# DeltaNet and a low-rank mixer on one core: the diagonal blocks of K K^T picked by ScalarE copies in five of eight units, with all queue orders drawn anew

## The chip, the cores and the metric

The kernel runs on one core of one Trainium2 chip. The metric is the time of one execution on the device, in microseconds (us). Engines: TensorE (PE, with its weight loads PEld), VectorE (DVE), ScalarE (ACT), GpSimd (POOL) and SyncE (SP), which only issues DMAs here. A verdict compares the medians of several executions of two kernels on the same chip.

## The reference

Two blocks follow each other: a DeltaNet recurrence over 4 batches, 8 heads, 768 tokens and head dimension 48, and a mixer over 384 channels with a low-rank token step (rank 32) and a two-layer channel step (384 to 1536 to 384). All in fp32.

```python
def _attn_ref(q, k, v, beta):
    k_n = k / (np.linalg.norm(k, axis=-1, keepdims=True) + 1e-06)
    state = np.zeros((B, H, D, D), dtype=np.float32)
    for t in range(S):
        kt, vt, bt = (k_n[:, :, t], v[:, :, t], beta[:, :, t, None])
        y[:, :, t] = np.einsum('bhd,bhde->bhe', q[:, :, t], state)
        v_old = np.einsum('bhde,bhd->bhe', state, kt)
        state = state + bt[:, :, :, None] * np.einsum('bhd,bhe->bhde', kt, vt - v_old)

def _moe_ref(x, U, V, w_ch1, w_ch2):
    xt = x.transpose(0, 2, 1)
    h = xt @ U @ V
    u = x + h.transpose(0, 2, 1)
    ch = np.maximum(u @ w_ch1, 0.0) @ w_ch2
    return u + ch
```

## The kernel before

**Units.** The recurrence is computed in chunks of 64 tokens (L = 64). A unit n (0 to 7) is half a batch: six chunks of all eight heads. Two slots of SBUF hold the units in turn. For each unit the kernel does this:

- `load` and `load_blocks`: DMAs of k, q, v and a second copy of k (called z), on the queues of SP and GpSimd.
- `norms`: norms of k, and the scaling of v.
- `grams(n, 0)` and `grams(n, 1)`: k (and q) are turned so that the head dimension lies on the partitions (TensorE transposes L668, or 32x32 VectorE transposes L690 in units 5 to 7), and TensorE forms K K^T (and K Q^T) per chunk in `products`, L704, for j = 0 and j = 1 (half of the heads each). A result is a [128, 2, 6, 64] block in two banks of PSUM (a "pair"). Of K K^T, each chunk's two 32x32 diagonal blocks are needed first. Rows sit in quarters of 32 partitions: quarters 0 and 2 hold the upper half of a chunk's rows, quarters 1 and 3 the lower half. So the upper diagonal block is columns 0 to 31 of quarters 0 and 2, the lower one columns 32 to 63 of quarters 1 and 3. They are collected in the tile `diag`: before, ScalarE multiplies columns 0 to 31 by a column `even[:, 0]` that is 1 in quarters 0 and 2 and 0 elsewhere (L714), and VectorE adds columns 32 to 63 times `even[:, 1]` (1 in quarters 1 and 3), in two instructions, r = 0 and 1 (L717). Then ScalarE copies the whole product to SBUF (L725).
- `blocks`: VectorE transposes `diag` into `gs` (L781), scales it, and inverts the 32x32 unit-triangular blocks by substitution, 31 steps of two instructions each (L790, L796; 15 steps in units 0 to 2, which split the blocks further). `joins` and `diagonals` then build the 64x64 inverses with small TensorE products, ScalarE copies (L926, L914) and GpSimd clears (L933).
- `recur(b)`: the 12 chunks of a batch in turn, each a chain from TensorE to VectorE or ScalarE and back: L1066 or L1107 (state times k), L1078 or L1120 (VectorE subtracts), L1090 and L1099 (ScalarE copies, units 2 to 7), L1135 (the update) and L1147 (VectorE adds it to the state). `outputs` and `put` (L972, L986, L956) give the chunk's rows of the mixer's input X.

**Mixer.** 12 blocks of 256 tokens. `front` does the low-rank step (L1469, L1486, added by VectorE in L1495) and transposes. The first seven blocks run `wide`: `channels`, six pieces each (L1580, or L393 in another form), a ReLU on ScalarE (L1545), then `narrow`, seven products with VectorE sums (L1695 or L393, added to X by VectorE in L1620). The last five blocks form the first layer in `products_of` (L1430) with fewer, precombined products. Weights come as fp64 bit patterns and are converted by VectorE and ScalarE in `convert` (L1244 to L1272). Results are stored by the SP queue (L1626, L1629).

**Order.** Nothing is scheduled at run time. Each part above is a generator that yields one step at a time, with the engine and a planned cost. The dictionary `ORDER` lists, for each engine, the number of the part whose step comes next; the loop `run` issues the steps in just that order, so each engine's queue is fixed. Parts are numbered as they are begun: 4 to 7 are `recur`; 8 to 11 are `norms`, `grams` for k, `grams` for q and `blocks` of unit 0, and 18 to 21, 30 to 33, 38 to 41 and so on by eight those of units 1, 2, 3 and on; `load` parts lie between them; 78 is the weights' load and conversion; 81 to 92 are `front`; 93 to 97 the first layer of the last five blocks; 98 to 109 `wide`. A number with points is a part begun by a part (39.0.0.0 is a `products` of unit 3, 102.2 the third `channels` piece of block 4). `PARTED` names the TensorE steps that are issued in quadrants: a 128x128 matmul is split into four of 64x64, which TensorE can interleave with the recurrence's 64-row products without a change of form.

The lines touched by the change are these: L714 and L717 in `products`; the steps that need its result, L781 (`blocks`) and L725; and all the strings of `ORDER`, with `PARTED`.

Of the kernel before, what the change touches and what calls it, by code (L numbers as in the profile page):

```python
# [15 lines left out]
L = 64  # L16
BK = 32
# [9 lines left out]
def kernel(  # L27
# [20 lines left out]
    nc = tc.nc  # L48
# [50 lines left out]
    def act(n):  # L99
        return 0.16 + n / 1200.0  # L100
# [27 lines left out]
    def advance(i, value, at):  # L128
# [20 lines left out]
        9.0 9.1 9.0.0.0 9.1.0.0 2*2 19.0 19.1 3 19.0.0.0 3 19.1.0.0 10.0 10.1 10.0.0.0 20.0 11.4 10.1.0.0  # L149
        11.4 11.2*2 11.4*2 11.2*2 20.1 11.4*4 20.0.0.0 11.2*4 20.1.0.0 4.1 4.0*2 4.1 21.2*2 4 4.4 21.2 4  # L150
        21.2 4.5 4 21.4*2 21.2 4 4.5 4.6 4*2 21.2 4.6 21.2*2 4.7 4*2 4.8 4.7 4 21.4 4.9 4 21.4 4 4.9 4.8
        4.2*2 21.4*2 4 4.10 21.4*2 4*2 4.10 4.11 4*2 4.11 4.3 32.0 31.0 4.3 31.1 4.12 4 31.0.0.0 31.1.0.0 4
        4.12 32.1 4.13 4*2 4.13 4.14 4 4.15 4 4.14 4.15 79 32.0.0.0 81 32.1.0.0 81*2 40.0 82 98.0*2 39.0
        39.1 82 98.1 40.1 39.1.0.0 39.0.0.0 98.1 98.2 33.2*2 98.2 98.3*2 98.4 33.4*2 33.2 98.4 33.2 98.5
        33.4*2 33.2*2 98.5 98.7 83 33.2 33.4 33.2 33.4 98.7 33.4*2 98.8 5 5.0 5 40.1.0.0 5 98.8 5.1 5 98.9 5
        98.9 5 5.1 98.9 5 98.9 5.2 5 98.10 5 5.2 5.3 5 99.0 5 99.0 5 5.3 5.4 5 99.0 5 99.0 5.5 5 99.1*2 5
        5.4 99.1*2 5.5 40.0.0.0 5 83 99.2*2 99.3*2 99.4 48.0 99.4 41.2*2 47.0 99.7 47.1 47.0.0.0 47.1.0.0
        41.4*2 99.5*2 48.1 41.2 41.4*2 41.2 99.7 99.8 48.1.0.0 5 99.8 5.6 5 48.0.0.0 5 99.9 5 99.9 5.7 5*2
        99.9 5 5.6 99.9 5.8 5.7 5 99.10 5*2 100.0 5.9 5 100.0 5.8 5 100.0 5 100.0 5.9 5 5.10 5 100.1 5.11 5
        5.10 100.1 5 5.11 100.1*2 84 100.2*2 100.3*2 100.4*2 100.5 100.7 100.5 49.2*2 55.0.0.0 84 55.1.0.0  # L160
        100.7 100.8 49.2 49.4*2 49.2 100.8 84 100.9*2 6 85 100.9 6 100.9 56.0.0.0 56.1.0.0 6 100.10 49.4*2
        6.0 6 101.0*2 85 6.1 6 101.1*2 6 101.1 6 101.1 6.2 6 101.2*2 6.1 6 101.2*2 6 6.3 6.2 101.3 6 101.3 6
        6.4 6.3 6 101.4 6 101.4 6.5 6 101.4 6 101.4 6.4 6 6.5 101.5*2 101.7*2 57.2*2 57.4*2 86 57.4*2 57.2*2
        101.8*2 101.9*2 63.0.0.0 101.10 6 101.10 6 63.1.0.0 102.0*2 86 6.6 6 102.1*2 64.0.0.0 6 6.6 102.2 6
        102.2 6.7 6 102.2*2 6 6.7 102.3 6 102.3 6.8 6 102.3 6 102.3 6.9 6 102.4 6 102.4 6.8 6 102.4 6 102.4
        6.10 6 102.5*2 6.9 6.11 102.5 6 102.5 6.10 6 102.7 6.11 102.7 87 102.7*2 64.1.0.0 87 102.8*2 102.9*2
        102.10 71.0.0.0 103.0*2 71.1.0.0 103.1*2 103.2*2 103.3*2 65.4*2 65.2*2 103.4*2 72.1.0.0 65.2*2
        65.4*2 103.5*2 87 103.7 7 72.0.0.0 7 103.7 7 7.0 103.8*2 7.1 7 103.8*2 7 88 7 103.9*2 7 7.1 7.2 7
        103.10 7 7.2 104.0 7 104.0 7.3 7 104.0*2 7 7.3 7.4 104.1 7 104.1 7 104.1*2 7.5 7 7.4 104.2 7 104.2
        88 104.3*2 7 7.5 73.4*2 73.2*2 104.4*2 104.5 73.4*2 73.2*2 104.5 7 104.7 7 7.6 7 104.7 7 7.7 104.8  # L170
        7.6 7 104.8 7 104.8 7 104.8 7 7.7 7.8 7 104.9 7 7.8 7.9 7 104.9 7 89 7 104.10 7 7.9 7.10 7 7.11 7
        104.10 7 7.10 7.11 79 93.2 93.1 79 89 93.4 93.2 93.1 93.3 93.2 93.3 93.4 93.1 93.5 93.1 93.2 93.1
# [12 lines left out]
        78.20*2 21.4 78.21 21.4 78.21*4 4 78.22*2 4 78.22*2 4 78.22 4 78.23*2 4 78.23*3 78.24*5 4 78.25*2
        31.0.0.0*2 31.1.0.0*2 4 33 4 30 4 78.25 4 33*2 4 78.25*2 33*2 78.26 32.0.0.0 78.26 81 33 78.26 81
        32.1.0.0*2 78.26 33 78.26 33 82 33*2 32.0.0.0 30 33*8 33.4 33.2 78.26.1*3 39.0.0.0 78.27 98.2.1*3
        39.1.0.0 78.26.1 39.0.0.0 30 78.27*4 39.1.0.0 33.2*3 33.4*2 78.27.1 33.4 41 98.5.1*2 78.27.1*2
        98.7.0 98.5.1 78.27.1 38 83 41 98.6 5 98.7.1 41*3 38 98.8.0 5 98.8.1 41*3 5 41 5 41*2 40.1.0.0
        98.9.0 41 98.9.1 5 40.1.0.0 41 98.10.0 5 41*2 5 41 5 41*2 5 41 5 41*15 41.2 5 99.2.1 40.0.0.0 99.2.1  # L190
        38 40.0.0.0 99.2.1 99.7.0 41.4 47.0.0.0*2 47.1.0.0*2 49 99.5.1*3 46 49*2 46 49*2 99.7.1 99.8.0 99.6
        5 48.1.0.0*2 99.8.1 49*2 48.0.0.0 5 48.0.0.0 49 5 49*2 5 49*2 5 99.9.0 49*2 99.9.1 49 99.10.0 5 49 5
        49*2 5 49 5 49*2 5 49 5 49*9 46 49*2 84 49 100.2.1*2 49.2 49.4 55.1.0 55.0.0 100.5.1*2 100.2.1
        100.5.1 100.7.0 84 55.1.0.0 55.0.0.0 55.1.0.0 100.7.1 55.0.0.0 100.6 57 100.8.0 54 100.8.1 56.0.0
        57*4 56.1.0 6 85 100.9.0 56.0.0.0 56.1.0.0 56.0.0.0 6 57 56.1.0.0 100.9.1 100.10.0 57*7 6 57 6 57*2
        6 57*2 6 57*3 101.2.1 57 6 57 6 57*2 6 57 6 57*5 6 54 57*3 57.2 101.2.1 101.7.0 57.4 101.2.1
        101.5.1*3 101.7.1 54 86 101.6 101.8.0 101.8.1 63.0.0 64.0.0 101.9.0 101.9.1 63.1.0 63.0.0.0 6
        63.0.0.0 101.10.1 101.10.0 64.1.0 63.1.0.0*2 65 62 65*2 6 65 64.0.0.0 62 6 64.0.0.0 65*2 6 65*2 6
        65*3 6 65 6 102.2.1 65 6 65 6 65*3 6 102.2.1*2 65 6 65 102.5.1*2 65 62 87 65 102.5.1 102.7.0 65*3
        102.7.1 65 102.8.0 65 102.6 102.8.1 87 65 102.9.0 65 71.0.0 65 102.9.1 102.10.0 64.1.0.0*2 71.1.0  # L200
        65*4 71.1.0.0 65 71.0.0.0 65.4 71.0.0.0 71.1.0.0 65.2 73 72.1.0 72.0.0 70 73*2 72.1.0.0 103.2.1 73
        72.1.0.0 73*3 103.2.1*2 73 103.7.0 103.5.1*2 72.0.0.0 73 7 103.5.1 103.7.1 73 72.0.0.0 7 73 103.6
        73*2 7 103.8.0 88 103.8.1 73 7 73*2 103.9.0 73*2 7 73 103.10.0 103.9.1 7 73*2 7 73*2 7 73*2 70 7
        73*3 7 73*6 73.2 73.4 7 70 80*3 104.2.1*2 80 104.2.1 104.5.1 7 80*2 93.0*2 104.5.1 7 104.7.0 104.5.1
        104.7.1 7 104.6 7*2 93.0 104.8.0 104.8.1 7 93.0 104.9.0 7 80 7 104.9.1 7 89 93.0 7*2 93.0*2 80
        93.0*2 80*2 93.0 80 104.10.0 80 93.2.1 94.0*3 80 93.1.1 93.0 80 93.3.1 93.2.2 93.1.2 93.1.3 104.10.1
        93.2.3 93.5.0 94.0 93.1.4 94.0*6 93.4.1 90 94.2.1 90 105.0*3 94.3.1 94.1.1 105.1 94.1.2 94.2.2
        105.1*2 105.3.1 105.3.0 95.0 94.1.3 95.0*4 94.5.0 94.2.3 95.0 105.4.0 94.0 105.2 94.4.1 95.0 105.4.1
# [209 lines left out]
    def quarter(i, size=BK):  # L418
        return slice(BK * i, BK * i + size)
# [1357 lines left out]
```

## Time and profile before

| quantity | us |
|---|---|
| median of 3 runs | 591.36 |
| lowest, highest | 589.72, 591.92 |
| profiled execution, its own time | 589.15 |
| its span in the trace | 587.4 |
| TensorE busy | 545.3 |
| VectorE busy | 456.2 |
| ScalarE busy | 227.3 |
| GpSimd busy | 118.1 |

How to read it: the span is from the first to the last event of the profiled execution, and the execution's own time has a little around it. A busy time is the time in which at least one instruction of the engine runs; TensorE's is the time of matmuls, whose weight loads (PEld) run beside them. The row of 40 digits cuts the span into slices of 14.7 us and gives the busy share in tenths; the row PEclk gives the clock that TensorE was granted, in tenths of full speed. An entry such as "PE P L972 <- DVE s L1147: 1.4, 3, 1.0" says that matmuls of line 972 waited 1.4 us in all, in 3 places, the longest 1.0 us, for VectorE's line 1147. Two instructions of one engine may overlap by some 0.1 us, so two instructions of 0.41 us can take 0.74 us together.

### The profile page before, as it was taken

The page shows a single profiled execution, that of the slowest core. Times are in us where ns is not written, and L with a number is a line of the kernel's source. Part 1 is how long each engine was busy: PE and PEld are TensorE (multiplying, and loading weights), DVE is VectorE, ACT ScalarE, POOL GpSimd, SP SyncE. Part 2 cuts the span into 40 slices and gives each one's busy share as a digit, 9 for nine tenths or more (in the row PEclk, how much of TensorE's full clock was granted, in tenths as well). Part 3 has the DMA queues.
Part 4 walks back from the last instruction along what each step waited for, and adds up shares of the span by engine and source line. Part 5 has one row for each costly group of instructions (what it writes and reads, how often), then busy time and mean ns, then how long its engine had stood idle before and what let it go on. Part 6 is the DMA issues. An engine that isn't in the chain of part 4 may idle for free.

```text
span 587.4 us, 25542 instructions
## 1 busy us (share of the span) xinstructions
PE 545.3 (93%) x11460; PEld 491.1 (84%) x11460; DVE 456.2 (78%) x1086; ACT 227.3 (39%) x483; POOL 118.1 (20%) x205
## 2 busy tenths in 40 slices
PE   5697778799999999999999999999999999999997
PEld 4586677588888987997897798988889999999997
DVE  6898999999899898899878888888547574555552
ACT  4447476544433623344344305324423422131220
POOL 8132050311205304340252253301000000000000
PEclk9576666799999999999999999999999999999999
DMA  9634676652104314223212433200000000000013
GB/s 157 85 76 128 192 188 166 134 91 63 29 4 83 68 22 83 74 53 63 48 30 61 80 75 71 60 29 3 2 5 1 2 1 1 1 2 1 1 42 119
DMA packets 79213, 35.17 MB, mean 60 GB/s; under 512 B 65600, under 2 KB 76992, under 8 KB 79104
## 3 DMA queue, kind: packets, MB, share of 16 engines
q1 hardware_dynamic: 71200, 24.10, 18.9%
q0 software_dynamic: 6304, 9.15, 7.2%
q8 instruction: 90, 1.47, 1.0%
q10 hardware_dynamic: 1600, 0.30, 0.3%
q14 instruction: 19, 0.16, 0.1%
HBM read 28.80 MB, written 4.72 MB: 57 GB/s over the span
## 4 chain that ended last, share of the span: by engine, by line
PE 79%; DVE 7%; ACT 5%; DMA 4%; issue 3%; SPq 1%; POOL 1%; DVEq 0%; ACTq 0%; POOLq 0%
PE P L1695 24%; PE P L1580 12%; PE P L1430 12%; PE P L393 10%; PE P L704 3%; DMA wide<-in_moe_w_ch_dram 2%; PE P L668 2%; PE P L1066 2%; PE P L1090 1%; PE P L972 1%; PE P L1486 1%; PE P L986 1%; PE P L1135 1%; PE P L1514 1%; PE P L861 1%
## 5 line engine op out<-in xcount | busy, mean ns | idle before, releaser
L1695 PE MATMUL P<-w_sb,hs 128*128 128x192 f32 x480 | 84.2, 329 | 0.1
L1580 PE MATMUL P<-ut,w_sb 128*128 128x256 f32 x348 | 81.8, 386 | 0.1
L1695 PEld LDWEIGHTS P<-w_sb,hs 128*128 128x128 f32 x480 | 77.7, 190 | 1.3 <-issue 0.3
L1580 PEld LDWEIGHTS P<-ut,w_sb 128*128 128x128 f32 x348 | 64.1, 190 | 9.4 <-issue 0.6
L796 DVE TENSOR_TENSOR xt<-xt,prod 128x112 f32<-128x112 f32 (+21 forms) x200 | 64.6, 323 | 6.9
L790 DVE TENSOR_TENSOR prod<-gs,xt 128x112 f32<-128x112 f32 (+21 forms) x200 | 63.7, 319 | 3.9
L1620 DVE TENSOR_TENSOR X<-X,P 128x192 f32<-128x192 f32 x86 | 29.6, 349 | 36.1 <-PE P L1695 34.2
L1545 ACT ACTIVATE hs<-P 128x512 f32<-128x512 f32 x42 | 24.8, 597 | 62.1 <-PE P L1580 51.0
L393 PE MATMUL P<-ut,w_sb 64*64 64x256 f32 x624 | 43.0, 384 | 1.2 <-ACT hs L1545 0.9
L956 ACT COPY X<-P 64x192 f32<-64x192 f32 x96 | 30.0, 312 | 28.8 <-PE P L986 27.2
L704 PE MATMUL P<-slot 48*64 48x64 f32 x1536 | 33.5, 245 | 1.9 <-ACT slot L682 1.6
L704 PEld LDWEIGHTS P<-slot 48*64 48x64 f32 x1536 | 30.0, 157 | 6.1 <-ACT slot L682 2.5
L933 POOL MEMSET slot<- 32x384 f32 x32 | 13.4, 420 | 102.6 <-PE P L890 40.4
L1412 DVE TENSOR_TENSOR hs<-hs,P 128x512 f32<-128x512 f32 x30 | 20.1, 684 | 17.5 <-PE P L1430 9.2
L1695 PE MATMUL P<-w_sb,S 128*128 128x192 f32 x192 | 33.7, 330 | 0.0
L926 ACT COPY slot<-zz 32x384 f32<-32x384 f32 x64 | 32.3, 508 | 1.0
L1099 ACT COPY z<-P 128x192 f32<-128x192 f32 x36 | 11.5, 319 | 53.3 <-PE P L1090 46.4
L1695 PEld LDWEIGHTS P<-w_sb,S 128*128 128x128 f32 x192 | 31.1, 190 | 0.6 <-DVE xt L796 0.3
L548 POOL DMA_DIRECT2D slot<-in_k_dram x44 | 28.7, 657 | 12.3 <-PE P L1135 10.6
L668 PE MATMUL P<-ident,slot 128*128 128x128 f32 x108 | 20.0, 343 | 11.3 <-DMA slot<-in_k_dram 5.7
L1430 PE MATMUL P<-slot 128*128 128x128 f32 x240 | 29.7, 276 | 0.0
L1695 PE MATMUL P<-w_sb,slot 128*128 128x192 f32 x168 | 29.1, 327 | 0.0
(171 smaller groups left out, 1140.9 us busy)
## 6 DMA issues: line engine op xcount, KB each, us to landing
out_dram<-X SPq DMA_DIRECT2D x22, 192.0 KB, 2.0
X<-in_moe_w_ch_dram SPq DMA_DIRECT2D x10, 384.0 KB, 4.4
wide<-in_moe_w_ch_dram SPq DMA_DIRECT2D x10, 384.0 KB, 4.4
slot<-in_k_dram SPq DMA_DIRECT2D x48, 72.0 KB, 3.7
slot<-in_k_dram POOLq DMA_DIRECT2D x44, 72.0 KB, 3.1
slot<-in_v_dram SPq DMA_DIRECT2D x32, 72.0 KB, 3.7
slot<-in_v_dram POOLq DMA_DIRECT2D x32, 72.0 KB, 3.2
hs<-in_moe_w_ch_dram SPq DMA_DIRECT2D x4, 384.0 KB, 5.7
```

What stands on the lines that cost most here:

```text
L393: nc.tensor.matmul(to[half(g)], w[half(r), half(g)], x[half(r)], start=start, stop=stop, skip_group_check=True,)
L548: queue.dma_start(out=t[half(1 - g if name == "z" else g), :, to, 0:D], in_=src[b, 4 * g + s, hf * UC * L : (hf + 1) * UC * L, :].rearrang ...
L668: nc.tensor.transpose(p_t[:, c // 3, c % 3], t[:, c, 2 * j : 2 * j + 2].rearrange("p s d -> p (s d)"), ident,)
L704: nc.tensor.matmul(p_g[half(g ^ (par * i)), par, c], kq[rows, c, j, 0, half(g)], kq[rows, c, j, i, half(g)], start=True, stop=True,)
L790: nc.vector.tensor_tensor(out=prod, in0=gb[:, :, j : j + 1, j + 1 :].to_broadcast([128, split, m, w]), in1=xb[:, :, 0:m, j : j + 1].to_bro ...
L796: nc.vector.tensor_tensor(out=xb[:, :, 0:m, j + 1 :], in0=xb[:, :, 0:m, j + 1 :], in1=prod, op=ALU.subtract,)
L926: nc.scalar.copy(pg[quarter(i), :, at, :, a : a + BK], cut(zc, h)[quarter(i)].rearrange("p r (c j) t -> p r c j t", j=2),)
L956: nc.scalar.copy(x[half(c % 2), c // 2, 4 * D * g : 4 * D * (g + 1)].rearrange("p (j r d) -> p r j d", r=2, d=D), states(p_y)[half(g)],)
L1430: nc.tensor.matmul(bank[:, q], w_block(w)[:, q // 2, 128 * (q % 2) : 128 * (q % 2) + 128], token(b, i, t), start=c == 0 and q == 0, stop=True,
L1580: nc.tensor.matmul(p_f[:, x], w(x, t), ut[:, t], start=(t == 0), stop=(t == KT - 1))
L1620: nc.vector.tensor_tensor(out=to, in0=to, in1=p, op=ALU.add)
L1695: nc.tensor.matmul(to, of[0], of[1], start=of[2], stop=of[3], skip_group_check=True)
```

## The change

In units 3 to 7 (`CORNERS`), `diag` is filled by ScalarE alone: a copy of columns 0 to 31 of all 128 partitions, and then, for quarters 1 and 3, a copy of columns 32 to 63 over it, 32 partitions each. Units 0 to 2 keep the multiplication and the two VectorE sums. All five strings of `ORDER` are new: 20 VectorE steps fewer and 20 ScalarE steps more for the picks, and other places for most other steps. In `PARTED`, 102.2 and 102.5 (two `channels` pieces) are no longer in quadrants and 103.10 (a last `narrow` product) is. `LATE` is only written with a space.

```diff
     SPLIT, QUARTERED = (0, 1), (2,)
+    CORNERS = range(3, 8)
...
             if i == 0:
                 to = diag[:, 0:CS].rearrange("p (r c j) t -> p r c j t", r=2, c=UC)[:, :, :, j]
                 yield op("act", act(384))
-                nc.scalar.mul(to, p_g[:, :, :, 0:BK], even[:, 0:1])
-                for r in range(2):
+                if n in CORNERS:
+                    nc.scalar.copy(to, p_g[:, :, :, 0:BK])
+                    for y in (1, 3):
+                        yield op("act", act(384))
+                        nc.scalar.copy(to[quarter(y)], p_g[quarter(y), :, :, BK:L])
+                else:
+                    nc.scalar.mul(to, p_g[:, :, :, 0:BK], even[:, 0:1])
+                for r in () if n in CORNERS else range(2):
                     yield op("dve", dve(192))
                     nc.vector.scalar_tensor_tensor(
```

The part of the new strings that the text speaks of, TensorE's start, the end of batch 0 and GpSimd's start, before and after:

```diff
-        9.0 9.1 9.0.0.0 9.1.0.0 2*2 19.0 19.1 3 19.0.0.0 3 19.1.0.0 10.0 10.1 10.0.0.0 20.0 11.4 10.1.0.0
+        9.0 9.1 9.0.0.0 9.1.0.0 2*2 19.0 19.0.0.0 10.0 10.1 3 10.0.0.0 20.0 3 10.1.0.0 19.1 19.1.0.0 11.2*2
...
-        4.12 32.1 4.13 4*2 4.13 4.14 4 4.15 4 4.14 4.15 79 32.0.0.0 81 32.1.0.0 81*2 40.0 82 98.0*2 39.0
+        4.13 32.1 4*2 4.13 4.14 4 4.15 4 4.14 4.15 79 32.0.0.0 81*2 32.1.0.0 81 98.0*2 82 40.0 98.1 39.0
...
-        11.0 13 23 78.0 2*3 17 23 25 23 13 23 25 13*2 25 29 25 21.0 15*2 29 17 15*2 11.3 11.1 11.3 11.1 27*4
+        2*2 13 23*2 13 11.0 13 2 78.0 17 13 23*2 25*2 21.0 25*2 15 27 29 15 17 29 15*2 27 11.3 27 11.1*2
...
-        81 86 19.0 40.0 98.9 99.0 99.1 99.9 100.0 100.1 100.9 101.1 101.2 101.4 101.10 102.2 102.3 102.4
-        102.5 102.7 103.8 104.0 104.1 104.8 104.10
+        81 86 19.0 40.0 98.9 99.0 99.1 99.9 100.0 100.1 100.9 101.1 101.2 101.4 101.10 102.3 102.4 102.7
+        103.8 103.10 104.0 104.1 104.8 104.10
```

ScalarE's queue around unit 6's picks (63.0.0.0 and 63.1.0.0; 6 is the recurrence, 102.0.0 a ReLU, 6.6 outputs, 57.3 the diagonals of unit 5), before and after:

```diff
-        101.4 6 101.4.0 6.4 6.5 6.4 6.5 101.5.0 57.4 57.2 57.1*2 57.2 57.1 57.4 57.2 57.1 63.0.0.0 57.3 57.4
-        57.3 6 63.1.0.0 63.0.0.0 63.1.0.0 62 86 57.3 102.1.0 102.0.0 6.6 6 102.2 102.2.0 57.3 6 6.6 102.3
+        6.5*2 101.5.0 57.1*3 57.4 57.2*3 57.4*2 57.1 57.3 63.0.0.0 6 63.0.0.0*3 63.1.0.0*4 102.0.0 62 6.6*2
+        57.3*2 6 57.3 102.1.0 86 102.2.0 6 102.3 102.3.0 6.8 6.7 6.8 6 102.4 6.7 102.4.0 6 6.9*2 102.5.0 6
```

## The prediction

> **What bounds the kernel now.** I read the page's head first, then the busy time by stretches, then TensorE's waits, then the lines that the change touches.
>
> ```profile
> span 587.4 us, 25542 instructions
> ...
> PE 545.3 (93%) x11460; PEld 491.1 (84%) x11460; DVE 456.2 (78%) x1086; ACT 227.3 (39%) x483; POOL 118.1 (20%) x205
> ...
> PE   5697778799999999999999999999999999999997
> ...
> DVE  6898999999899898899878888888547574555552
> ...
> PEclk9576666799999999999999999999999999999999
> ```
>
> Two regimes. Up to slice 8 (14.7 us each) VectorE is at 8 to 9 tenths, TensorE at 5 to 8, and its clock is half granted. From there to the end TensorE is full. The stretches give the numbers (columns: length, then busy time of PE, PEld, DVE, ACT, POOL, the granted clock, DMA):
>
> ```profile
> 80.00:100.00 20.00, 14.74 (x491) 13.15 (x487) 19.31 (x31) 12.16 (x25) 7.77 (x12) 0.69 0.78 183
> 100.00:120.00 20.00, 15.26 (x531) 12.20 (x533) 18.31 (x41) 10.16 (x21) 7.58 (x12) 0.83 0.71 136
> 120.00:440.00 320.00, 313.25 (x7628) 271.68 (x7620) 269.66 (x660) 125.08 (x292) 78.84 (x134) 1.00 0.23 49
> 440.00:585.00 145.00, 144.14 (x1147) 141.17 (x1139) 79.58 (x181) 35.43 (x64) 0.00 (x0) 1.00 0.05 17
> ```
>
> Before 120 us VectorE is the limit (18 to 19 of 20 us busy). After 120 us TensorE stands idle for only 320 - 313.25 = 6.75 us, and after 440 us for about nothing. VectorE with 269.66 of 320 (84%) is a close second there. What TensorE waits for between 120 and 440 us:
>
> ```profile
> PE P L972 <- DVE s L1147: 1.4, 3, 1.0
> PE P L393 <- ACT hs L1545: 1.1, 4, 0.4
> PE P L986 <- ACT z L1099: 1.0, 2, 0.5
> PE P L1135 <- ACT z L1099: 0.9, 3, 0.5
> PE P L1066 <- DVE s L1147: 0.6, 1, 0.6
> ```
>
> With two smaller rows (0.2 on VectorE, 0.3 on ScalarE) that is 2.2 us on VectorE and 3.3 us on ScalarE. So the engine that is relieved holds TensorE up less than the engine that gets the work. That caps the idea of the change.
>
> The lines that it touches, all eight units (columns: busy, mean ns of one, idle before):
>
> ```profile
> L717 DVE SCALAR_TENSOR_TENSOR slot<-P,even,slot 128x192 f32<-128x192 f32 x32 | 11.8, 406 | 3.1 <-ACT slot L714 3.1
> L714 ACT ACTIVATE slot<-P,even 128x384 f32<-128x384 f32 x16 | 9.2, 579 | 18.2 <-PE P L704 18.0
> L725 ACT COPY slot<-P 128x768 f32<-128x768 f32 x16 | 12.7, 801 | 7.8 <-DVE slot L717 7.6
> L926 ACT COPY slot<-zz 32x384 f32<-32x384 f32 x64 | 32.3, 508 | 1.0
> L914 ACT ACTIVATE slot<-P 32x384 f32<-32x384 f32 x32 | 15.2, 479 | 7.6 <-PE P L908 7.3
> ```
>
> And one place of it, unit 6, ScalarE and then VectorE:
>
> ```profile
> 307.48 0.58 ACT L714 ACTIVATE slot<-P,even 128x384 f32<-128x384 f32 x1 [0.34 <-PE P L704]
> 308.08 1.67 ACT L725 COPY slot<-P 128x768 f32<-128x768 f32 x2
> ...
> 308.21 0.70 DVE L717 SCALAR_TENSOR_TENSOR slot<-P,even,slot 128x192 f32<-128x192 f32 x2
> 309.02 1.97 DVE L781 STREAM_TRANSPOSE gs<-slot 128x1024 f32<-128x1024 f32 x1
> ```
>
> The pick is 0.58 us on ScalarE, two times 0.35 us on VectorE, then the transposition L781, which starts the unit's substitution.
>
> **The change, part by part.** Base: the profiled execution took 589.15 us, its span 587.4 and 1.75 around it; the median of the runs is 591.36, so 2.2 us above the profiled one. I add changes to the median.
>
> *Removed from VectorE.* Five units, two products each, two L717 each: 20 instructions. Back to back two take 0.70 to 0.74 us, so 0.33 to 0.41 each: 6.6 to 8.2 us, of which I take 6.8. They stand between 134 and 360 us, where TensorE is full. They shorten the end only through the 2.2 us that TensorE waits there for VectorE, and the waited-for instruction (L1147, 0.35 us) is itself part of that wait. Bounds: 0 (all of it is turnaround) and -6.75 (every gap closes, since some ScalarE waits start late because VectorE was late). I take half of 2.2: -1.1.
>
> *Added on ScalarE.* L714 becomes a plain copy of the same shape (0.48 to 0.58). Two copies of 32x384 come behind it, from PSUM; no row shows just that. L926 has the shape from SBUF at 0.51, L914 the shape from PSUM at 0.48; bounds 0.48 and 0.58 (L714), plus up to 0.1 because the first quarter copy waits for the copy below it on its own engine. I take 0.5, by L914 and L926: 20 x 0.5 = 10 us (9.6 to 13.6). Cover: ScalarE is idle 195 of 320 us there. If the cover were gone all 10 to 11 us would show. The new wait on VectorE's side is nil: L781 waits for ScalarE about 1 us longer per product and for 0.7 us less of its own work. Queued behind the copies on ScalarE: in unit 6, the big copy L725 of both products, the relu L1545 of block 102 (it frees a bank for L1580), the output copies L956 and the next state copy L1099, and TensorE waits for the last three. ScalarE's load rises by 10 of 125, 8%; in proportion its 3.3 us of TensorE waits rise by 0.3; at worst unit 6 holds a state copy for 4.2 us (0.8 + 0.8 big copies, 0.58 and four times 0.5). I take +0.5, nearest to proportion, since the other four units' products lie where no recurrence step is in flight. Against it, L725 waited 7.6 us for L717 in five places, and those of them that fall in units 3 to 7 go. The Trainium skill, "PSUM — Partial Sum Buffer", PSUM bank collisions, says two engines must not read one bank in the same partitions at once, and software keeps them apart; that would explain this row, which alone does not say why a copy waits for another reader. By that rule ScalarE gets back part of what it is given, and the sum would be without the +0.5.
>
> *Queues drawn anew: the front.* I gave each entry of VectorE's queue the time that it took in this trace and added up what stands ahead of a given entry. Ahead of the last subtraction of batch 0's recurrence (L1120 at 110.9 us): 94.8 us before, 93.8 in the new order. Ahead of the first low-rank addition (L1495 at 117.8): 101.0, now 97.7. TensorE's work ahead of the first block's L1469 (113.5 us) is 82.4 us in both. So the recurrence ends 1.0 us earlier at VectorE's pace, and the addition could come 3.3 us earlier, but not ahead of the recurrence. Between them TensorE waits 1.3 us for L1495 (118.83); in the new order a group of L704 (1.2 us) stands in that gap. I take -1.0 for the recurrence and -1.0 of the 1.3: -2.0. Bounds -4.3 and, if the clock below goes the other way, +3.7.
>
> *Queues: loads.* On GpSimd the clearing of xt falls behind six DMA issues (two of 0.6, four of 0.66), from 2.8 to about 6.6 us; its first user starts at 15.3 us, so 7.7 us of cover. The load of U moves from 5.2 to about 8.3 us and lands 5.5 us after, near 14; its first user now stands behind L781 (13.0 to 15.0): 0 to 0.3 us. On TensorE the second half of unit 1's k, for which it stood idle 4.9 us at 15 to 20 us, falls behind 9 us of unit 0's q; that stretch is VectorE's, so 0. The price: unit 1's substitution ends with 3.7 us more VectorE work ahead (L803 at 52.6), but its result is needed at 81 us behind 8 us of slack. The SP queue issues unit 1's k, z and the weights in another order, with the same bytes; 0. At the end six stores of 0.46 us each stand between the last block's first store and its next (5.9 us apart): 0.
>
> *TensorE itself.* Two channel pieces (102.2, 102.5) go from quadrant to full form: L1580 x12 takes 2.79, the four pieces of L393 1.1 + 0.62 + 1.1 + 0.62 less four overlaps of 0.18 take 2.7. One last product (103.10) goes to quadrants: 2.2 to 2.0. Sum 0, within 0.3.
>
> Sum: -1.1 + 0.5 - 2.0 + 0 = -2.6, so 591.36 - 2.6 = 588.8 us.
>
> **Rivals.** Half a percent, 2.96 us, is about what a measurement of this kernel tells from no change: faster is below 588.4, slower above 594.3.
>
> *Relief in full.* TensorE's idle 6.75 us are turnarounds behind a crowded VectorE; with 6.8 us less work 60% of them go (-4.0), and the front takes its full 3.3: 591.36 - 7.3 = 584.1. For it: by the same adding up, VectorE's work ahead of every milestone from 157 us on shrinks by 2 to 8 us while TensorE's stays. Against: the waits listed on VectorE are only 2.2.
>
> *ScalarE takes VectorE's place (slower).* The copies hold L1099, L956 and L1545 back, in units 4 and 6 above all, where recurrence steps are near. If 7 of the 11 us are uncovered: 591.36 - 2.0 - 1.1 + 7 = 595.3. It decides from about 6 us uncovered. For it: ScalarE's share of TensorE's waits. Against: its 61% idle time.
>
> *The clock.* Before 120 us the granted clock is 0.55 to 0.85. If the slice 100 to 120 were granted 0.67, as 20 to 40 was, its 15.26 x 0.83 = 12.7 us of full-clock work would take 19.0 instead of 15.3: +3.7 in place of -2.0, 591.36 - 0.6 + 3.7 = 594.5. The Trainium skill, "TensorE: Matmul & The Clock Gate", What's actually happening, says the gate looks at free-running windows of 3413 ns, halves the clock after an idle one and frees it after a busy one; the rows with two levels agree, and by it one more halved window costs 1.7 us, which makes the sum 590.5.
>
> *Nothing.* The relief is hidden and the front's first wait only moves: 591.4.
>
> **How the numbers follow.** Forecast (587 to 591) 0.48; relief in full 0.18; ScalarE 0.14; clock 0.12; nothing 0.08. Of the forecast's share 0.22 lies below 588.4. Faster 0.18 + 0.22 = 0.40; same 0.26 + 0.08 = 0.34; slower 0.26. The range must reach both outer groups: 584.0 to 595.0 leaves out half of the first and of the ScalarE case, about 0.16.
>
> **What would show it.** Right: L717 x12 instead of x32, 20 new 32x384 copies near 0.5 us; VectorE near 449 us busy, ScalarE near 237; TensorE's first full stretch (first L1580) 1 to 3 us before 121.5; idle of TensorE from there to 440 us between 5 and 7. Wrong: more than 10 us of such idle with rows naming L1099 or L1545 (ScalarE), a granted clock below 0.80 in 100 to 120 us (clock), or idle below 4 us (relief in full).

## The result and the profile after

The changed kernel is slower. On the chip of the prediction: 596.91 us (median of 4 runs, 595.17 to 598.6) against 591.22 for the kernel before, a ratio of 1.0100 with a 95% interval of 1.0064 to 1.0135. Measured again later, on another chip, 12 runs against 35: 596.42 against 593.10, ratio 1.0046 (1.0016 to 1.0075). One of the 35, at 597.83 us, counts as a slow run and is left out of the ratio. Weighted by their intervals the two give about 1.0068, some 4 us. The prediction was 588.8, in a range of 584.0 to 595.0.

The profiled execution of the changed kernel took 595.17 us. Head of its page:

```profile
span 593.5 us, 25461 instructions
...
PE 555.8 (94%) x11424; PEld 502.3 (85%) x11424; DVE 449.8 (76%) x1067; ACT 234.4 (40%) x500; POOL 118.9 (20%) x205
...
PE   5786987889999999999999999999999999999997
...
DVE  5969999988989888879978887888666564545452
...
PEclk9999999999999999999999999999999999999999
```

VectorE lost 6.4 us of work (456.2 to 449.8) and ScalarE gained 7.1 (227.3 to 234.4), as the edit says. TensorE is busy 10.5 us longer with fewer instructions, and nearly all of it comes ahead of the first L1469 (the first low-rank product), where both kernels have the same matmuls. The stretch up to there, before and after (columns as in the prediction):

```profile
0.00:113.50 113.50, 82.74 (x2562) 74.62 (x2562) 101.23 (x234) 65.65 (x126) 33.41 (x62) 0.70 0.63 140
```

```profile
0.00:118.10 118.10, 92.58 (x2563) 84.92 (x2563) 99.14 (x234) 65.04 (x125) 33.48 (x62) 0.99 0.61 133
```

TensorE needed 9.8 us more for the same matmuls, so more of them ran at a lower clock. The row PEclk shows nothing of it, and it can't be believed in this profile. Two rows of TensorE's timeline in the changed kernel, the same 48 products in the same shape:

```profile
23.35 1.56 PE L702 MATMUL P<-slot 48*64 48x64 f32 x48
...
121.12 0.88 PE L702 MATMUL P<-slot 48*64 48x64 f32 x48
```

The first took 1.8 times as long, at a clock recorded as full. By the length of such groups, TensorE changed between half and full clock here too until about 120 us, as it did in the kernel before.

The lines that the edit touches (groups by line and form):

```profile
L729 ACT COPY slot<-P 128x768 f32<-128x768 f32 x16 | 12.7, 793 | 0.6 <-DVE slot L721 0.2
L716 ACT COPY slot<-P 32x384 f32<-32x384 f32 x20 | 9.3, 471 | 0.4
L713 ACT COPY slot<-P 128x384 f32<-128x384 f32 x10 | 4.8, 480 | 22.3 <-PE P L702 22.3
L721 DVE SCALAR_TENSOR_TENSOR slot<-P,even,slot 128x192 f32<-128x192 f32 x12 | 4.4, 412 | 4.2 <-ACT slot L718 4.2
L718 ACT ACTIVATE slot<-P,even 128x384 f32<-128x384 f32 x6 | 3.5, 582 | 6.1 <-PE P L702 6.1
```

(Line numbers are 4 higher than before from L717 on, and 2 or 3 lower ahead of it: L717 is now L721, L704 is L702.) The sums are 12 instead of 32; the quarter copies take 471 ns each; the big copy L729 waits 0.2 us for VectorE where L725 had waited 7.6.

The stretches and TensorE's waits from the first channel step (124 us) to the last recurrence step (445 us):

```profile
100.00:120.00 20.00, 17.00 (x543) 14.38 (x541) 17.05 (x38) 12.80 (x24) 3.32 (x6) 0.91 0.53 141
120.00:440.00 320.00, 311.95 (x7533) 271.03 (x7535) 268.25 (x646) 133.49 (x308) 83.50 (x141) 1.00 0.26 52
440.00:585.00 145.00, 144.01 (x1288) 140.27 (x1281) 80.55 (x181) 35.90 (x67) 0.00 (x0) 1.00 0.04 13
```

```profile
PE P L390 <- ACT hs L1549: 1.3, 4, 0.6
PE P L1094 <- DVE w L1082: 1.2, 4, 0.4
PE P L1139 <- ACT z L1103: 1.1, 3, 0.6
PE P L1584 <- ACT ut L1521: 0.9, 1, 0.9
PE P L1070 <- DVE s L1151: 0.5, 2, 0.3
```

Between the first channel step and the last recurrence step TensorE stood idle 6.47 us (320.16 less 313.69 busy), where it had been 6.74: where the picks are, hardly anything was won or lost. The starts of some steps show where the time went (us; before's lines are named):

| start of | before | after | difference |
|---|---|---|---|
| unit 1's first L781 | 29.83 | 34.15 | +4.3 |
| last L1120 of batch 0 | 110.89 | 115.78 | +4.9 |
| first L1469 | 113.50 | 118.10 | +4.6 |
| last channel step of the first wide block | 145.61 | 150.96 | +5.4 |
| last L1090 | 439.54 | 444.46 | +4.9 |
| last output product, L1695 | 582.27 | 588.31 | +6.0 |

So in these two executions nearly the whole loss is there before 118 us, ahead of every pick that was changed, and about 1 us comes behind 440 us. In the front VectorE, which should have come through faster, has less to do and waits more. Its 20 to 40 us, before and after:

```profile
20.00:40.00 20.00, 18.80 (x433) 17.27 (x434) 18.39 (x53) 9.68 (x19) 4.78 (x7) 0.67 0.38 67
```

```profile
20.00:40.00 20.00, 18.27 (x314) 16.69 (x316) 14.91 (x42) 11.53 (x22) 2.89 (x4) 1.00 0.46 107
```

The third busy time is VectorE's: 18.39 and 14.91 of 20 us. What it waited for from 0 to 62 us, before and after:

```profile
DVE slot L679 <- PE P L668: 2.4, 2, 1.5
...
DVE norm L614 <- ACT norm L611: 0.5, 1, 0.5
DVE slot L717 <- ACT slot L714: 0.2, 1, 0.2
```

```profile
DVE slot L721 <- ACT slot L718: 4.0, 3, 1.9
DVE slot L677 <- PE P L666: 3.3, 2, 2.1
DVE norm L612 <- ACT norm L609: 2.2, 1, 2.2
```

These three kinds of wait add up to 3.1 us before and 9.5 after, and all of VectorE's waits in this stretch to 6.7 and 12.5, so 5.8 us more: VectorE now stands still for products' first copies, turned k and q, and a norm, which TensorE and ScalarE deliver.

### The profile page after: what moved, and what is told of

Its sections match the earlier page's. It is cut to its first block, busy times and chain, and to the rows that moved or that the text cites. A ratio compares the mean times of both kernels' runs of the same rounds, so it can differ in the third digit from the quotient of the medians.

```text
span 593.5 us, 25461 instructions
## 1 busy us (share of the span) xinstructions
PE 555.8 (94%) x11424; PEld 502.3 (85%) x11424; DVE 449.8 (76%) x1067; ACT 234.4 (40%) x500; POOL 118.9 (20%) x205
## 4 chain that ended last, share of the span: by engine, by line
PE 82%; DVE 9%; ACT 3%; DMA 3%; issue 2%; POOL 1%; SPq 0%; DVEq 0%; ACTq 0%
PE P L1699 23%; PE P L1584 14%; PE P L1434 12%; PE P L390 10%; PE P L702 4%; PE P L666 2%; PE P L1094 2%; PE P L865 2%; PE P L851 2%; PE P L1070 2%; PE P L1490 1%; PE P L990 1%; PE P L976 1%; PE P L1139 1%; PE P L1518 1%
## 5 line engine op out<-in xcount | busy, mean ns | idle before, releaser
L1584 PE MATMUL P<-ut,w_sb 128*128 128x256 f32 x372 | 87.6, 385 | 1.1 <-ACT ut L1521 0.9
L1699 PE MATMUL P<-w_sb,hs 128*128 128x192 f32 x468 | 81.7, 329 | 0.8 <-DVE X L1624 0.5
L1699 PEld LDWEIGHTS P<-w_sb,hs 128*128 128x128 f32 x468 | 75.9, 190 | 2.6 <-issue 1.4
L1584 PEld LDWEIGHTS P<-ut,w_sb 128*128 128x128 f32 x372 | 68.3, 190 | 10.8 <-ACT ut L1521 1.1
L960 ACT COPY X<-P 64x192 f32<-64x192 f32 x96 | 30.1, 313 | 27.6 <-PE P L990 26.5
L390 PE MATMUL P<-ut,w_sb 64*64 64x256 f32 x528 | 37.2, 385 | 1.8 <-ACT hs L1549 1.3
L702 PE MATMUL P<-slot 48*64 48x64 f32 x1536 | 34.1, 247 | 4.1 <-ACT slot L680 4.0
L702 PEld LDWEIGHTS P<-slot 48*64 48x64 f32 x1536 | 30.7, 159 | 7.0 <-ACT slot L680 4.9
L1434 PE MATMUL P<-slot 128*128 128x128 f32 x240 | 30.3, 277 | 0.0
L1434 PEld LDWEIGHTS P<-slot 128*128 128x128 f32 x240 | 28.7, 192 | 0.4
L1103 ACT COPY z<-P 128x192 f32<-128x192 f32 x36 | 11.5, 319 | 42.1 <-PE P L1094 40.2
```

The costliest lines, as they stand in the source:

```text
L390: nc.tensor.matmul(to[half(g)], w[half(r), half(g)], x[half(r)], start=start, stop=stop, skip_group_check=True,)
L702: nc.tensor.matmul(p_g[half(g ^ (par * i)), par, c], kq[rows, c, j, 0, half(g)], kq[rows, c, j, i, half(g)], start=True, stop=True,)
L960: nc.scalar.copy(x[half(c % 2), c // 2, 4 * D * g : 4 * D * (g + 1)].rearrange("p (j r d) -> p r j d", r=2, d=D), states(p_y)[half(g)],)
L1434: nc.tensor.matmul(bank[:, q], w_block(w)[:, q // 2, 128 * (q % 2) : 128 * (q % 2) + 128], token(b, i, t), start=c == 0 and q == 0, stop=True,
L1584: nc.tensor.matmul(p_f[:, x], w(x, t), ut[:, t], start=(t == 0), stop=(t == KT - 1))
L1699: nc.tensor.matmul(to, of[0], of[1], start=of[2], stop=of[3], skip_group_check=True)
```

## The experiments

The change has two parts, the picks and the queues. Theory A: the queues lose the time, first of all in the front. Rival B: ScalarE's copies lose it. The runs then cut the new order into stretches. A cut is made in the order in which the steps are issued: up to a named step every queue follows the one kernel, behind it the other.

**picks_alone.** The old queues; only the 20 sums leave VectorE's string and 20 copies come into ScalarE's, each directly behind its product's first copy:

```diff
-        ... 57.2 63.0.0.0 57.3 57.4 57.3 6 63.1.0.0 63.0.0.0 63.1.0.0 62
+        ... 57.2 63.0.0.0*3 57.3 57.4 57.3 6 63.1.0.0*3 63.0.0.0 63.1.0.0 62
```

> The queues of before, with only the pick changed in units 3 to 7: the two VectorE sums of a product are taken out of VectorE's queue, and the two quarter copies stand directly behind the first copy in ScalarE's. Theory A (the loss comes from the order of the first 120 us): the picks are neutral, 590 to 592 us against 591.2 of before, VectorE's busy time 6 to 7 us less. Theory B (ScalarE's copies hold the recurrence up): 594 to 597 us, with more TensorE idle time naming L1099 or L1545's counterparts after 120 us.

Measured: 592.52 us (10 runs) against 592.27, ratio 1.0008 (0.9988 to 1.0027). VectorE was busy 450.1 us, ScalarE 235.6: the whole exchange of work, and no change that can be measured (at most 1.6 us by the interval). B falls. One thing stood in its trace that was not in the kernel before, at the last recurrence step (TensorE's timeline, before and then picks_alone):

```profile
440.45 0.45 PE L986 MATMUL P<-z,slot 64*64 64x48 f32 x16 [0.25 <-ACT z L1099]
440.83 2.05 PE L1430 MATMUL P<-ut,w_sb 128*128 128x128 f32 x16
```

```profile
441.25 0.45 PE L990 MATMUL P<-z,slot 64*64 64x48 f32 x16 [0.25 <-ACT z L1103]
442.78 1.49 PE L1434 MATMUL P<-ut,w_sb 128*128 128x128 f32 x11 [1.08 <-ACT X L960]
```

The order is the same. But PSUM pairs are handed out when the program is built, by the planned times, and those had moved a little: the last two output products got pairs 0 and 1 in place of 2 and 1, and the mixer's first product L1434 takes pair 0 next. So it waits 1.1 us for the copy L960. (The next expectation calls the product in pair 0 the last one; it is the last but one.)

**picks_clean.** The same, with those two products kept off pair 0:

```diff
-    def opens(s):
+    def opens(s, i):
         banks, of = places(s)
+        of = [x for x in of if i not in ("7.10", "7.11") or 0 not in x]
```

> The old queues with the new picks alone, as in the first of these runs, but the last two output products of the recurrence are kept off PSUM pair 0. (In that first run's trace the last one lay in pair 0, which the first blocks' mixing takes next, and TensorE waited 1.1 us there for its copy; the kernel before has it in pair 1 and waits for nothing.) Theory A (the picks relieve a little and that 1.1 us hid it): 0.3 to 1.2 us below before. Rival (the relief is worth nothing at all): within 0.3 us of before.

Measured: 592.33 us (12 runs) against 593.10, ratio 0.9990 (0.9967 to 1.0013), and the 1.1 us wait is gone. The middle of it agrees with theory A, -0.6 us, but the interval, -2.0 to 0.8, holds zero: what the picks are worth is not separated from nothing.

**front_before and front_after.** The changed kernel with the old order up to the second step of part 81 (`front`, block 98; its first step is the first L1469), and the kernel before with the new order up to its first step.

```diff
-        9.0 9.1 9.0.0.0 9.1.0.0 2*2 19.0 19.0.0.0 10.0 10.1 3 10.0.0.0 20.0 3 10.1.0.0 19.1 19.1.0.0 11.2*2
+        9.0 9.1 9.0.0.0 9.1.0.0 2*2 19.0 19.1 3 19.0.0.0 3 19.1.0.0 10.0 10.1 10.0.0.0 20.0 11.4 10.1.0.0
...
-        4.13 32.1 4*2 4.13 4.14 4 4.15 4 4.14 4.15 79 32.0.0.0 81*2 32.1.0.0 81 98.0*2 82 40.0 98.1 39.0
+        4.12 32.1 4.13 4*2 4.13 4.14 4 4.15 4 4.14 4.15 79 32.0.0.0 81 32.1.0.0 81*2 98.0*2 82 40.0 98.1
```

(TensorE's string in front_before against the changed kernel; front_after is the reverse, on the kernel before.)

> The changed kernel, but every queue keeps the order of before up to TensorE's second step of the first low-rank block (about 116 us); behind that the new order. Theory A: the 4.6 us that the new order had lost by then come back, 591.5 to 593 us (of the 5.7 us the last 1.1 us, lost after 440 us, stay). Theory B: the new picks are all there, so 596 to 597 us.

> The kernel before, with the old picks, but with the new order of all queues up to the first low-rank block (about 116 us). Theory A: 595 to 596.5 us. Theory B: 591 us, since none of the new ScalarE copies is in it.

Measured: front_before 596.72 us (5 runs), ratio 1.0077 (1.0027 to 1.0126); front_after 594.91 (10 runs), 1.0052 (1.0026 to 1.0078); before 592.27. Put into the kernel before, the new front costs about 3.1 us (1.5 to 4.6), a little less than theory A expected. Taken out of the changed kernel it gives nothing that can be seen: theory A expected 591.5 to 593 us of front_before, and it came out where the changed kernel is, 1.6 to 7.5 us above the kernel before. So A was at best incomplete, and the rest was cut further.

**start_before and start_after.** The same two cuts, but already at unit 1's first L781 (about 30 us). TensorE's string of start_after against the kernel before:

```diff
-        9.0 9.1 9.0.0.0 9.1.0.0 2*2 19.0 19.1 3 19.0.0.0 3 19.1.0.0 10.0 10.1 10.0.0.0 20.0 11.4 10.1.0.0
-        11.4 11.2*2 11.4*2 11.2*2 20.1 11.4*4 20.0.0.0 11.2*4 20.1.0.0 4.1 4.0*2 4.1 21.2*2 4 4.4 21.2 4
+        9.0 9.1 9.0.0.0 9.1.0.0 2*2 19.0 19.0.0.0 10.0 10.1 3 10.0.0.0 20.0 3 10.1.0.0 19.1 19.1.0.0 11.2*2
+        11.4*4 11.2*2 20.1 11.4*4 20.0.0.0 11.2*4 20.1.0.0 4.1 4.0*2 4.1 21.2*2 4 4.4 21.2 4 21.2 4.5 4
```

> The changed kernel, with the order of before only up to VectorE's transposition of unit 1's diagonal blocks (about 30 us, so with unit 1's k turned ahead of unit 0's q), and the new order from there. If the loss is made in the start (VectorE's and TensorE's waits between 13 and 34 us): 591.5 to 593.5 us. If it is made between 34 and 118 us by other changes of order: 595 to 597 us.

> The kernel before, with the changed kernel's order in every queue only up to VectorE's first transposition for unit 1 (about the first 30 us; on TensorE unit 0's q ahead of the second half of unit 1's k), and the old picks. Theory A (the front's loss, measured as +2.6 us with the whole new front, is made in these 30 us): 2 to 3 us above before, unit 1's transposition at about 34 us and its return near 60 us in place of 52.6. Rival C (the loss is made between 30 and 81 us, by VectorE's and ScalarE's later order, or is the clock's chance): within 1 us of before.

Measured: start_before 595.39 us (8 runs), ratio 1.0045 (1.0015 to 1.0075), so not the 591.5 to 593.5 of a loss that the start alone makes; its trace has 0.8 us in the wait at pair 0. start_after 595.83 (11 runs) against 593.09, ratio 1.0066 (1.0036 to 1.0096), of which its trace shows 1.4 us in the wait at pair 0. That leaves about 2.5 us (0.7 to 4.3), as much as the whole front costs, so by the runs of start_after the first 30 us make it. The traces do not bear this out. The execution of start_after (592.09 us, the shortest of the 11) has unit 1's L781 at 31.99 in place of the 34 expected, and the first L1469 only 1.1 us late. And VectorE's waits up to 62 us, 6.7 us before and 12.5 after, are 6.8 in it and 10.6 in start_before: they follow the order behind the first 30 us, not the one in them.

**k1_first and k1_clean.** The changed kernel with the second half of unit 1's k ahead of unit 0's q again, the second with the pairs mended:

```diff
-        9.0 9.1 9.0.0.0 9.1.0.0 2*2 19.0 19.0.0.0 10.0 10.1 3 10.0.0.0 20.0 3 10.1.0.0 19.1 19.1.0.0 11.2*2
+        9.0 9.1 9.0.0.0 9.1.0.0 2*2 19.0 19.0.0.0 19.1 19.1.0.0 10.0 10.1 3 10.0.0.0 20.0 3 10.1.0.0 11.2*2
...
-        10.0.0 10.1.0 78.14.0 19.0.0.0 20.0.0 19.0.0.0*2 3 19.1.0 3 19.1.0.0 11.4.0 11.2 19.1.0.0 11.4.0
+        19.1.0 19.1.0.0 10.0.0 10.1.0 78.14.0 19.0.0.0 20.0.0 19.0.0.0*2 3*2 11.4.0 11.2 19.1.0.0 11.4.0
```

> The changed kernel with one thing put back: on TensorE the second half of unit 1's k stands ahead of unit 0's q again, and ScalarE's norm copies follow. Theory A: the changed kernel's loss of 4.5 to 5.7 us over before shrinks by 2.0 to 2.6 (2.0 to 3.5 us above before), since VectorE's wait for unit 1's blocks goes. Rival C: it stays at 4.5 us or more above before.

> The changed kernel with the second half of unit 1's k put back ahead of unit 0's q on TensorE and ScalarE, and the two output products kept off pair 0. Theory A1 (unit 0's q ahead of it is what costs in the start): 2 to 2.6 us below the changed kernel. Rival A2 (the start's loss is the whole new order of these 30 us, VectorE's and the loads' too): less than 1.2 us below it.

Measured: k1_first 597.42 us (6 runs), ratio 1.0087 (1.0058 to 1.0116); k1_clean 597.19 (12 runs), 1.0067 (1.0043 to 1.0090), beside 596.42 for the changed kernel. Nothing comes back. The swap that the prediction named, by itself, is not the cause; which part of the new front is stays open.

**mid81.** The queues of picks_alone, with the new order only from the second step of part 81 to the first step of 98.8 (by the trace of before, from about 117 to 153 us; the expectation below sets the beginning at 97 us, but TensorE's string first differs at this step):

```diff
-        ... 79 32.0.0.0 81 32.1.0.0 81*2 40.0 82 98.0*2 39.0
+        ... 79 32.0.0.0 81 32.1.0.0 81*2 98.0*2 82 40.0 98.1
```

> The old queues with the new picks, but the changed kernel's order in every queue from the second of TensorE's three weight-combination steps (97 us) up to the first state step of block 98's second half (about 155 us). Theory A (a second loss is made right behind the first low-rank block, where TensorE is given three waiting products in a row and its clock falls back): 1 to 3 us above before, half-speed products between 112 and 130 us. Rival D (that stretch only follows the clock's chance): within 0.8 us of before.

Measured: 595.04 us (12 runs) against 593.09, ratio 1.0036 (1.0016 to 1.0056), 2.1 us (0.9 to 3.3), of which the trace has 1.1 in the wait at pair 0. TensorE's timeline there, before and then after the change:

```profile
116.70 0.82 PE L1486 MATMUL P<-tt,v_sb 64*64 64x192 f32 x16
118.83 0.93 PE L405 MATMUL P<-ident,X 64*64 64x64 f32 x48 [1.31 <-DVE X L1495]
119.58 1.11 PE L405 MATMUL P<-ident,slot 64*64 64x64 f32 x48
120.68 0.88 PE L1486 MATMUL P<-tt,v_sb 64*64 64x192 f32 x16
121.49 2.86 PE L1580 MATMUL P<-ut,w_sb 128*128 128x256 f32 x12
```

```profile
120.42 0.88 PE L1490 MATMUL P<-tt,v_sb 64*64 64x192 f32 x16 [0.52 <-DVE tt L1480]
121.12 0.88 PE L702 MATMUL P<-slot 48*64 48x64 f32 x48
122.45 0.93 PE L402 MATMUL P<-ident,X 64*64 64x64 f32 x48 [0.45 <-DVE X L1499]
124.30 2.86 PE L1584 MATMUL P<-ut,w_sb 128*128 128x256 f32 x12 [0.92 <-ACT ut L1521]
```

Before, the one wait of 1.31 us is followed by 2 us of other products (a turn of unit 3's k, 1.11, and the next L1486, 0.88), and under these ScalarE's copy of x is made (L1521 after the change, L1517 before). After, L702 fills part of the first gap, but those two products stand behind the channel step: TensorE turns x, has nothing else, and waits 0.92 us for the copy. The wait was split and moved; 1.3 us became 1.9. mid81 has the same 0.92. The half-speed products that its expectation named do not tell the orders apart: the clock's record has TensorE at half for 10.3 us there in mid81, and for 10.2 in picks_alone, which has the old order.

**tail_after.** The kernel before, with the new order behind the last recurrence step:

```diff
-        104.10 7 7.10 7.11 79 93.2 93.1 79 89 93.4 93.2 93.1 93.3 93.2 93.3 93.4
+        104.10 7 7.10 7.11 79 93.1 89 93.2 79 93.4 93.3 93.1 93.2 93.3 93.2 93.1
```

> The kernel before, with the changed kernel's order in every queue only behind the last recurrence step (from about 440 us). Theory A (a third loss in the tail: last block's first product waits 0.5 us for VectorE, about 0.8 us of small gaps behind the recurrence): 1.0 to 1.9 us above before. Rival: within 0.5 us of before, the difference in the two traces being only a shift of what was late already.

Measured: 593.74 us (12 runs) against 593.09, ratio 1.0019 (0.9997 to 1.0041), 1.1 us at the middle. Its waits on TensorE from 441 us on have one that the kernel before has not:

```profile
PE P L971 <- DVE s L1146: 1.0, 1, 1.0
PE P L1694 <- DVE X L1619: 0.5, 1, 0.5
```

The last block's first output product waits for VectorE's addition to X, which the new order put late. The stretch from the last L1090 to the last output product takes 143.87 us in its trace, 143.84 in both traces of the changed kernel and 142.73 before: +1.1, of which 0.5 is this wait; what makes the other 0.6 is not shown.

**repaired_clean.** The new picks, the old order up to about 160 us and behind 440, the new order between, with the pairs mended (shown against the changed kernel).

```diff
-        9.0 9.1 9.0.0.0 9.1.0.0 2*2 19.0 19.0.0.0 10.0 10.1 3 10.0.0.0 20.0 3 10.1.0.0 19.1 19.1.0.0 11.2*2
+        9.0 9.1 9.0.0.0 9.1.0.0 2*2 19.0 19.1 3 19.0.0.0 3 19.1.0.0 10.0 10.1 10.0.0.0 20.0 11.4 10.1.0.0
...
-        104.10 7 7.10 7.11 79 93.1 89 93.2 79 93.4 ...
+        104.10 7 7.10 7.11 79 93.2 93.1 79 89 93.4 ...
```

> The new picks; the old order in every queue up to about 160 us and behind the last recurrence step (440 us), the changed kernel's order between them; the same two output products kept off pair 0. Theory A (the whole loss was made in three places, the first 30 us, the stretch behind the first low-rank block, and the tail): within 1 us of before, more likely below. Rival (the new order between 160 and 440 us costs too): 1.5 us or more above before.

Measured: 591.93 us (12 runs) against 593.10, ratio 0.9993 (0.9969 to 1.0016). With the three stretches undone the loss is gone, and the new order from 160 to 440 us costs nothing that can be measured (at most 0.9 us by the interval). It is no version that beats the kernel before by more than can be measured.

**after_again.** The changed kernel as it is, beside the last three.

> The changed kernel itself beside these, on the same chip, for a sum of the parts: 5 to 6 us above before by its first four runs; the parts measured alone (start 2.4 to 2.6, behind the first low-rank block about 1, tail about 0.7, picks 0 to -0.6) add up to 3.5 to 4.3.

Measured: ratio 1.0046, as told above. The parts, from the runs with the pair's wait taken off: front 2.5 to 3.1, behind the first low-rank block 1.0, tail 1.1, picks -0.6, in all 4.0 to 4.6 us, beside 2.7 and 5.9 us for the whole in its two measurements (4 pooled). Each part has an interval of 1 to 2 us either way, and without the pair's wait only the front's excludes zero, so the agreement is a loose one.

The traces of all these runs, cut at three steps (us; "old" and "new" are the order ahead of the first L1469, and behind it; "waits" are all of VectorE's in the first 62 us; "TensorE busy" is up to the first L1469, for 2562 to 2566 matmuls in every run):

| run | front, behind | waits | TensorE busy | first L1469 | to the last channel step of the first wide block | to the last L1090 | to the last output product |
|---|---|---|---|---|---|---|---|
| before | old, old | 6.7 | 82.7 | 113.5 | 32.1 | 293.9 | 142.7 |
| picks_alone | old, old | 6.4 | 83.9 | 114.5 | 31.7 | 294.1 | 143.9 |
| picks_clean | old, old | 6.5 | 85.2 | 115.9 | 31.4 | 294.2 | 142.7 |
| tail_after | old, old | 6.4 | 85.4 | 115.9 | 32.7 | 294.5 | 143.9 |
| repaired_clean | old, old | 7.4 | 85.2 | 118.1 | 32.2 | 294.3 | 142.7 |
| mid81 | old, new | 7.2 | 86.6 | 117.7 | 33.3 | 294.2 | 143.9 |
| front_before | old, new | 6.9 | 86.7 | 118.5 | 35.5 | 294.1 | 144.7 |
| front_after | new, old | 10.1 | 84.8 | 115.4 | 34.2 | 293.4 | 142.7 |
| after | new, new | 12.5 | 92.6 | 118.1 | 32.9 | 293.5 | 143.8 |
| after_again | new, new | 14.1 | 92.2 | 120.6 | 34.4 | 293.3 | 143.8 |
| start_after | new to 30 us, old | 6.8 | 82.9 | 114.6 | 32.4 | 294.0 | 144.2 |
| start_before | old to 30 us, new | 10.6 | 84.1 | 115.1 | 35.1 | 293.9 | 144.7 |
| k1_first | new but the swap, new | 10.6 | 86.8 | 117.6 | 33.8 | 294.0 | 144.7 |
| k1_clean | new but the swap, new | 13.1 | 89.2 | 118.7 | 32.9 | 293.1 | 144.0 |

Two things can be read from it. VectorE's waits go with the order: 6.4 to 7.4 us in the eight traces with the old order from 30 us on, 10.1 to 14.1 in the six with the new. And with one and the same order, that of the first seven rows, the first L1469 moves by 5 us, later, with one exception, as TensorE takes longer for the same matmuls: that part goes with the clock.

## Why the prediction was wrong

*VectorE's relief, -1.1.* picks_clean measures this term and the next together: forecast -0.6, measured -0.6 at the middle, in an interval that holds zero. The traces show no gain: the stretch to the last L1090 takes 293.9 us with the old picks and 294.1 and 294.2 with the new alone. The prediction itself had a reason: the waits that VectorE makes there end with L1147, which is part of the turnaround. picks_alone still has most of them, 1.0 us for the outputs' products (1.4 before) and 0.6 for the recurrence's (0.6).

*ScalarE's copies, +0.5.* The cost was right, 471 ns each for the 0.5 taken, 9.3 us for 10; the +0.5 that TensorE should wait did not show: its waits for ScalarE, without the one for L1521, come to 3.2 us in the changed kernel for 3.3 before. A wait on VectorE's side that the prediction took as nil is there, 1.5 us of L785 (L781 before) for L716 in two places; it costs nothing that can be seen. In unit 6 (ScalarE's timeline of the changed kernel) the planned order let the state copy L1103 in between:

```profile
309.44 0.48 ACT L713 COPY slot<-P 128x384 f32<-128x384 f32 x1 [6.26 <-PE P L702]
309.91 0.32 ACT L1103 COPY z<-P 128x192 f32<-128x192 f32 x1
310.26 0.96 ACT L716 COPY slot<-P 32x384 f32<-32x384 f32 x2
311.24 0.80 ACT L729 COPY slot<-P 128x768 f32<-128x768 f32 x1
```

The 4.2 us for which a state copy might have been held did not come. By the rule cited there (the Trainium skill, "PSUM — Partial Sum Buffer", PSUM bank collisions: two engines must not access one bank in the same partitions at the same time) L725's wait for VectorE would go where VectorE no longer reads. It went, 7.6 to 0.2 us, and earned nothing that can be seen; ScalarE is busy only 40% of the time.

*The front, -2.0: the step that failed.* "So the recurrence ends 1.0 us earlier at VectorE's pace ... I take -1.0 for the recurrence and -1.0 of the 1.3: -2.0." Both halves were wrong. By the runs the new front costs 2.5 to 3.1 us in place of gaining 2.0. The last L1120 came at 115.78, 118.29 and 113.38 us in the three traces with the new front (mean 115.8) and at 110.89 to 115.91 in the seven with the old one (mean 113.7), +2.1 in place of -1.0; these overlap, so the runs are the stronger evidence. And the wait for L1495 did not shrink by 1.0; with the wait that took its place it grew by 0.6. The method was to add up what stands in VectorE's queue ahead of a step. That is a lower bound of when the step can run, and it becomes the time only if the engine never waits longer than it did. VectorE did have less to do ahead of the last L1120, 97.0 us busy in place of 98.7; but it stood idle 18.8 us there in place of 12.2, and its waits up to 62 us are longer in every trace with the new order behind 30 us. The second premise, TensorE's 82.4 us of work in both, failed too: at the clock that the changed kernel's two executions got, it took 92.6 and 92.2 us.

*The swap of q and k and the loads, 0.* "That stretch is VectorE's, so 0." By the runs of start_after the new order of this stretch costs about 2.5 us, so the 0 was wrong, though the traces put VectorE's longer waits in the order that follows. The item that the text named, the second half of unit 1's k behind unit 0's q, gave nothing when it was put back. Its price was named but taken too small: unit 1's blocks came back not 3.7 but 9.3 us later (52.57 to 61.88), beyond the 8 us of slack that were given. Yet front_after has them at 59.31 and reaches the first L1469 at 115.4, earlier than most old fronts, so this one trace does not show the lateness of unit 1 to be the loss in itself.

*The end, 0.* +1.1 in the traces, 0.5 of it by an addition of VectorE put behind other work; only SP's stores were looked at there.

*TensorE itself, 0.* Nothing against it: the same stretch holds the pieces that changed form, and it stays within 0.8 us of before in all the other traces.

*The base.* The prediction added its changes to the median, but read its waits and its turning points from one execution. Of seven profiled executions with this same front, that one was the earliest at the first L1469 (113.5; the others 114.5 to 118.5). What the trace showed as a front with one wait was also the luckiest one.

*The rivals.* The ScalarE rival and the full relief fall. The clock rival named the right stretch and came near the size (594.5), and the same matmuls did take 9.8 us more ahead of the first L1469. Its form, 0.67 in 100 to 120 us, did not come: 0.91 in the first profile, whose record begins only at 105.8, and 0.76 in after_again. Its sign, a clock below 0.80 there, does not tell the kernels apart either: picks_alone has 0.74 and loses nothing. "Nothing" fits the picks and is wrong for the queues. The case that happened, new waits in the front from another engine's order, was not among them.

**What stays open.** Which moves of the front cost the time: the runs of start_after point to the first 30 us, the traces to the order behind them, and no run mixes single queues of the two kernels there. And how much of the front's loss is the half clock: some of VectorE's longer waits are for products that ran at half clock, and TensorE took 92 us for its matmuls in both profiles of the changed kernel, but 84.8 in front_after, which has the same front. Whether the order brings the half clock on or these executions met it by chance, no run shows.

## What to carry to other kernels

A queue's summed work ahead of a step bounds it from below; before it counts as a gain, list for each engine what the first steps wait for and whether the producer moved back in its own queue. When an order is drawn anew as a whole, price every stretch of it, also where the edit isn't: here the edit was worth nothing that could be measured, and three stretches away from most of it made the loss. And where buffers are handed out by a planned time, an edit can move a buffer hundreds of microseconds later; look for waits that the order alone does not explain.

## What the runs showed of the hardware

The same program on the same chip takes between 588.63 and 595.57 us (34 runs of the kernel before), and the traces place most of it ahead of the first L1469: that step starts between 113.5 and 118.5 us in seven traces of one order, while the stretch of 294 us that begins at about 146 us differs by 1.4 us over all fourteen. TensorE goes between half and full clock there in steps of 3.4 us or a multiple: in the trace of before at 10.6, 14.0, 31.1, 37.9, 55.0 and 61.8 us, and on to 116.4. In the six traces with the old front and a whole record (all but front_before) the mean clock of the first 130 us falls from 0.72 to 0.67, and the first L1469 comes at 113.5 us with 0.72 and at 117.7 with 0.67 (the latest, at 118.1, has 0.68). The Trainium skill, "TensorE: Matmul & The Clock Gate", HAM oscillation — how this bites in real kernels, describes a TensorE that waits over 3.4 us between bursts and is slowed each time. This front is slowed again and again too, but at shorter waits: from 20 us on TensorE stands idle at most 2.7 us at a time in the trace of before, and it is 74 to 94% busy in stretches of 20 us.

The record of the clock can be missing: the changed kernel's two profiles begin theirs at 105.8 and 62.5 us and show full clock until then, while groups of 48 equal products take from 0.88 to 1.56 us. The same page of the Trainium skill, Seeing it yourself, warns that these events were unreliable; here the length of a fixed group is the better clock.
